# The clock that places pairs of scores among an FFN's passes: two constants for an exponential instead of one

## The chip, the cores and the metric

The kernel runs on one core of one Trainium2 chip. The metric is the device time of one execution in microseconds (us). Five engines take part: TensorE (PE in the profile; PEld is its loading of weights, which overlaps matmuls), VectorE (DVE), ScalarE (ACT), GpSimd (POOL) and SyncE (SP, which issues most DMAs). Each engine takes its own instructions in order, and waits on the others by semaphores.

## What is computed

One transformer layer on 2048 tokens of width 576: normalisation and attention with 32 query heads that share one key and value head of 18 columns, then a second normalisation and a bilinear FFN with 4608 hidden columns, both with a residual.

```
q = (x @ wq).reshape(B, S, H, Dh).transpose(0, 2, 1, 3)
k, v = x @ wk, x @ wv
scores = einsum("bhqd,bkd->bhqk", q, k) * (Dh ** -0.5)
p = softmax(scores, axis=-1)
o = einsum("bhqk,bkd->bhqd", p, v)
h = A_x + o.transpose(0, 2, 1, 3).reshape(B, S, H * Dh) @ wo      # x above is layernorm(A_x)
g = einsum("bsd,df->bsf", layernorm(h), w_gate)
u = einsum("bsd,df->bsf", layernorm(h), w_up)
out = h + einsum("bsf,fd->bsd", g * u, w_down)
```

## The kernel before

The tokens are cut into four blocks of 512 queries. Attention of a block is 8 groups of 4 heads; a group takes 16 tiles of 128 keys, and a tile takes two **pairs** of scores. A pair (`pair`, `scores`, L628 and L629) is two matmuls of 56 rows that run side by side, into one of two PSUM tiles `s` (128 x 1024), and one exponential on ScalarE from there into a tile `P` in SBUF, of which there are seven. There are 1024 pairs. **Values** (`values`, L633) are eight matmuls that read the two P tiles of a key tile and add into `acc`; one such visit ends the use of both P tiles. `flush` issues the visits that are due; `pend` holds the key tiles whose pairs are issued and whose values are not, `half` an odd pair.

The FFN of a block (`ffn`) goes over 36 tiles of 128 hidden columns, here called steps. A step has 27 **passes** (L991): two matmuls side by side, for the gate (`pg`) and the up half (`pu`), from 64 rows each. Weights and activations are split in a high and a low part, hence three products for each of nine chunks. ScalarE then copies `pg` to `g` (L1008), VectorE multiplies with `pu` to `hf` (L1013), and the result is split in high and low parts by casts on ScalarE and subtractions on VectorE (`room`, L92 and L93). After every second step a down product (`down`, L936, 42 matmuls on `y`) with a scheme of seven products for a two by two split follows one step late.

TensorE has 282 pairs done before the FFN of block 0 begins; the other 742 are put among the passes of blocks 0 and 1, since TensorE would otherwise have to wait for ScalarE's exponentials. When the last pair is out, blocks 2 and 3 run their passes without any (there the two halves are named `gu`).

Where a pair goes is decided when the program is written, by a clock in microseconds that the code keeps. `t_pe` is TensorE's time: 0.23 for a pass and for a pair, 0.893 for a visit of values, and so on. `t_act` is ScalarE's. `ends[n]` is the time at which pair n's exponential is held to be done, and so its PSUM tile to be free. Ahead of every pass `pace` asks `room_for_pair`: a pair n goes in when pair n - 2 is done by `t_pe`, and when fewer than eight pairs wait for their values. `paced` moves the clock after a pair. An eighth pair has no P tile until the next visit of values; it is kept in `late`, and its exponential's time is set in `flush`. Values are due behind the thirteenth pass of a step and behind the last; behind the seventh too, where a group's last key tile is the first due. After each group of visits the next two pairs go in at once, as both PSUM tiles are free by then.

Three casts on ScalarE are issued at fixed passes of a step: that of the first hidden half behind the sixth pass of odd steps (`left_first`, 128 x 256), that of the sums behind the ninth pass of even steps (`left_sums`, 128 x 1024), and attention heads at times behind the fifteenth (`run_aux`). ScalarE takes them in the order in which the code issues them, between exponentials.

Of the kernel before, what the change touches and what calls it, by code (L numbers as in the profile page):

```python
# [57 lines left out]
class Block:  # L58
# [545 lines left out]

    def paced(self, n):

        self.t_pe += T_PAIR
        if len(self.pend) * 2 + len(self.half) > P_BUFS + (self.p2 is not None):
            self.late[n] = len(self.late)
        else:  # L610
            self.t_act = self.ends[n] = max(self.t_act, self.t_pe) + T_EXP

    def room_for_pair(self):

# [21 lines left out]
    def flush(self, n):  # L636

        if n:
            self.t_pe += T_SWITCH
        for b, g, t, Ps in self.pend[:n]:  # L640
            self.t_pe += T_VISIT
            for k in sorted(self.late)[:2]:
                del self.late[k]
                self.t_act = self.ends[k] = max(self.t_act, self.t_pe) + T_EXP
            if t == 0:
                self.acc = self.ps_acc(b, g)
            self.values(self.acc, Ps, t)
            if t == NT - 1:
                os_ = self.os[g] = self.op.tile([P, TB], F32, tag="os", bufs=1, name=f"os{b}_{g}")
                self.dve.transpose(os_, self.acc)  # L650
                self.aux.insert(0, (self.round + 1, lambda b=b, g=g, o=os_: self.normalise(b, g, o), None))
        del self.pend[:n]
# [577 lines left out]

RATE = 2.3

T_PASS, T_PAIR, T_VISIT, T_SWITCH, T_EXP, T_DOWN = 0.23, 0.23, 0.893, 0.2, 1.05, 5.85
P_BUFS = 6

P1, P2, P3, P4, P5, P6, P7 = (0, 0), (1, 1), (6, 2), (2, 6), (3, 3), (4, 4), (5, 5)
# [128 lines left out]
```

## Time and profile before

| | us |
|---|---|
| median of three runs | 2394.43 (2392.9 to 2395.39) |
| the profiled execution | 2392.47 |
| its span, from the first to the last instruction | 2390.7 |

The profile is of one execution. A row of a group reads: line, engine, operation, tiles out<-in, shapes, count | busy us, mean ns of one | idle time ahead of them and what ended it. The chain of waits is the work that ended last, followed back; each of its rows has a start, the time it holds on the chain, and the work. The end of a matmul is modelled: a matmul that starts to load weights late is drawn longer, so a busy TensorE need not run at its peak.

### The profile page before, as it was taken

To read this page: it belongs to the slowest core of one execution; us is meant where nothing else is said; L and a number is where in the kernel's file an instruction comes from. 1 tells how busy PE (TensorE), PEld (TensorE's weight loads), DVE (VectorE), ACT (ScalarE), POOL (GpSimd) and SP (SyncE) were. 2 spreads that over 40 slices of the span, in tenths; PEclk is the share of its full clock that TensorE was granted. 3 is DMA by queue.
4 is the path that set the end of the run, shared out by engine and by line. 5 is a ranking of instruction groups with operands and counts; after the bars stand their busy time and mean duration, and the time that the engine had idled before them with its cause. 6 is when DMAs were issued, how large, how long until landed. Compare 5 with 4: busy or idle time off the path is not lost.

```text
span 2390.7 us, 46004 instructions
## 1 busy us (share of the span) xinstructions
PE 2335.7 (98%) x18102; PEld 1563.2 (65%) x18102; DVE 1168.8 (49%) x2047; ACT 1405.7 (59%) x1868; POOL 647.4 (27%) x802
## 2 busy tenths in 40 slices
PE   7999999999999999999999999999799999999999
PEld 5333344666666666666666566667687888888888
DVE  7565543334343453344444433334566656566565
ACT  6888877766776677666676777775122323233232
POOL 5445301212212212212212122122232433334333
PEclk9999999999999999999999999999899999999999
DMA  5778733323323323353333233233544554655543
GB/s 175 259 255 290 259 131 106 115 84 109 121 85 115 105 93 118 100 163 117 99 103 115 76 111 121 83 103 123 175 144 142 191 186 169 204 177 190 181 164 125
DMA packets 158289, 345.41 MB, mean 144 GB/s; under 512 B 16845, under 2 KB 48461, under 8 KB 158069
## 3 DMA queue, kind: packets, MB, share of 16 engines
q1 hardware_dynamic: 155333, 331.16, 42.3%
q0 software_dynamic: 2736, 11.26, 1.5%
q8 instruction: 145, 2.38, 0.4%
q14 instruction: 75, 0.61, 0.1%
HBM read 272.45 MB, written 55.67 MB: 137 GB/s over the span
## 4 chain that ended last, share of the span: by engine, by line
PE 83%; DVE 2%; issue 1%; ACT 1%; DMA 0%; POOL 0%; DVEq 0%; SPq 0%; ACTq 0%; POOLq 0%
PE gu L991 19%; PE pg L991 17%; PE y L936 17%; PE acc L633 15%; PE s L628 11%; PE yo L774 3%; PE pu L991 1%; PE y L894 1%; ACT P L629 1%; DVE room L93 0%; PE ye L894 0%; DVE hf L1013 0%; ACT g L1008 0%; DMA q<-q_dram 0%; DVE ws L93 0%
## 5 line engine op out<-in xcount | busy, mean ns | idle before, releaser
L629 ACT ACTIVATE P<-s 128x1024 f32<-128x1024 f32 x1024 | 992.3, 1027 | 337.1 <-PE s L628 290.1
L944 POOL TENSOR_TENSOR h<-h,tmp 128x288 f32<-128x288 f32 x408 | 316.3, 808 | 924.7 <-ACT tmp L943 924.1
L991 PE MATMUL pu<-X,ws 64*128 64x512 f32 x1890 | 524.0, 390 | 0.0
L991 PE MATMUL pg<-X,ws 64*128 64x512 f32 x1890 | 523.9, 390 | 0.0
L633 PE MATMUL acc<-P,V 128*32 128x512 f32 x4096 | 500.4, 600 | 0.1
L991 PE MATMUL gu<-X,ws 64*128 64x512 f32 x3996 | 470.7, 391 | 3.3 <-DMA X<-X 2.3
L628 PE MATMUL s<-q,kT 56*128 56x512 f32 x2048 | 431.4, 441 | 8.7 <-ACT P L629 4.5
L991 PEld LDWEIGHTS gu<-X,ws 64*128 64x128 f32 x3996 | 382.7, 185 | 81.4 <-issue 8.4
L936 PE MATMUL y<-wdo,room 128*128 128x288 f32 x2856 | 409.1, 300 | 0.9 <-DVE h L939 0.9
L936 PEld LDWEIGHTS y<-wdo,room 128*128 128x128 f32 x2856 | 386.8, 188 | 31.8 <-issue 24.4
L628 PEld LDWEIGHTS s<-q,kT 56*128 56x128 f32 x2048 | 183.3, 184 | 328.0 <-ACT P L629 177.5
L991 PEld LDWEIGHTS pg<-X,ws 64*128 64x128 f32 x1890 | 350.0, 186 | 69.8 <-issue 2.0
L939 DVE TENSOR_TENSOR h<-h,y 128x288 f32<-128x288 f32 x544 | 235.8, 454 | 246.1 <-PE y L936 242.4
L991 PEld LDWEIGHTS pu<-X,ws 64*128 64x128 f32 x1890 | 350.0, 186 | 3.0 <-DVE hf L1013 0.2
L943 ACT COPY tmp<-y 128x288 f32<-128x288 f32 x408 | 162.9, 400 | 261.4 <-PE y L936 247.5
L92 POOL CAST ws<-wr 128x1152 fp32r<-128x1152 f32 x144 | 168.4, 1171 | 502.8 <-PE pu L991 352.5
L1013 DVE TENSOR_TENSOR hf<-pu,g 128x512 f32<-128x512 f32 x70 | 48.4, 692 | 434.0 <-ACT g L1008 434.0
L633 PEld LDWEIGHTS acc<-P,V 128*32 128x32 f32 x4096 | 105.8, 109 | 236.1 <-issue 213.0
L93 DVE TENSOR_TENSOR ws<-wr,ws 128x1152 fp32r<-128x1152 f32 x144 | 196.8, 1367 | 61.3 <-POOL ws L92 61.3
L1008 ACT COPY g<-gu 128x512 f32<-128x512 f32 x74 | 43.7, 590 | 197.8 <-PE gu L991 197.8
L92 ACT CAST room<-hf 128x256 fp32r<-128x256 f32 (+1 forms) x144 | 75.1, 521 | 95.7 <-DVE hf L1013 95.5
L93 DVE TENSOR_TENSOR room<-S,room 128x1024 fp32r<-128x1024 f32 x68 | 83.3, 1225 | 91.8 <-ACT room L92 91.7
(171 smaller groups left out, 1474.7 us busy)
## 6 DMA issues: line engine op xcount, KB each, us to landing
wdo<-wd_dram SPq DMA_DIRECT2D x492, 288.0 KB
wr<-in_wgu_dram SPq DMA_DIRECT2D x144, 576.0 KB
wd_dram<-wd_room SPq DMA_DIRECT2D x20, 1008.0 KB
q<-q_dram SPq DMA_DIRECT2D x64, 216.0 KB
q_dram<-qs SPq DMA_DIRECT2D x16, 504.0 KB
X<-X SPq DMA_DIRECT2D x28, 256.0 KB
wd_dram<-wd_hi SPq DMA_DIRECT2D x7, 1008.0 KB
wd_dram<-wd_src SPq DMA_DIRECT2D x7, 1008.0 KB
```

What stands on the lines that cost most here:

```text
L92: (copy or self.cast)(hi, src)
L93: self.dve.tensor_tensor(lo, src, f32(hi), ALU.subtract)
L628: self.pe.matmul(s_[:, i], self.kT[o:o + 56, t * P:(t + 1) * P], q[o:o + 56, pr], start=True, stop=True)
L629: self.act.activation(p_, s_, AF.Exp, scale=SCALE)
L633: self.pe.matmul(acc[32 * j:32 * j + 32, :], self.V[:, t, :], Ps[j // 2][:, j % 2, :], start=(t == 0), stop=(t == NT - 1), skip_group_chec ...
L774: pe.matmul(y[:, :HD], m, k, start=(i == 0), stop=(i == len(ms) - 1))
L936: pe.matmul(y[:, :HD], m[:, t * P:(t + 1) * P], k, start=(first and j == 0), stop=(j == 2), skip_group_check=True)
L939: dve.tensor_tensor(hs, hs, y[:, :HD], ALU.add)
L943: act.copy(z, y[:, :HD])
L944: pool.tensor_tensor(hs, hs, z, ALU.add)
L991: pe.matmul(ps, w[o:o + 64, wk, c], X[o:o + 64, xk, c], start=(j == 0), stop=(j == 26))
L1013: dve.tensor_tensor(hf, pu, g, ALU.mult)
```

## The change

`paced` and `flush` now share a method, and one constant for an exponential becomes three. Before, an exponential was held to start when its pair's own 0.23 us were over (or the one ahead of it was done), and both ScalarE and the PSUM tile were held to be free 1.05 later. Now it is held to start 0.6 after the pair's start (or when ScalarE can take it), ScalarE can take the next one 0.92 after that, and the PSUM tile is free 1.09 after that. For a pair with ScalarE idle the tile is thus held free 1.69 after the pair's start, where it was 1.28; for exponentials one behind another the distance is 0.92, where it was 1.05. Nothing is computed otherwise, and no instruction is added or taken out.

```diff
     def paced(self, n):
 
+        ready = self.t_pe + T_READY
         self.t_pe += T_PAIR
         if len(self.pend) * 2 + len(self.half) > P_BUFS + (self.p2 is not None):
-            self.late[n] = len(self.late)
+            self.late[n] = ready
         else:
-            self.t_act = self.ends[n] = max(self.t_act, self.t_pe) + T_EXP
+            self.exp_ends(n, ready)
+
+    def exp_ends(self, n, ready):
+
+        start = max(self.t_act, ready)
+        self.t_act, self.ends[n] = start + T_EXP, start + T_FREE
@@ flush
             for k in sorted(self.late)[:2]:
                 del self.late[k]
-                self.t_act = self.ends[k] = max(self.t_act, self.t_pe) + T_EXP
+                self.exp_ends(k, self.t_pe + T_READY)
@@
-T_PASS, T_PAIR, T_VISIT, T_SWITCH, T_EXP, T_DOWN = 0.23, 0.23, 0.893, 0.2, 1.05, 5.85
+T_PASS, T_PAIR, T_VISIT, T_SWITCH, T_READY, T_EXP, T_FREE, T_DOWN = 0.23, 0.23, 0.893, 0.2, 0.6, 0.92, 1.09, 5.85
```

All other functions are as before, and so is the order of instructions up to the FFN of block 0. In its steps, and in those of block 1, the pairs stand at other passes. TensorE's order in two steps of block 0 that follow each other, before and after (`.` a pass, `S` a pair, `V` a visit of values, `D` a down product):

```
even step, before  ....S....S...S..VVSS....S....S...S...VVVSSDSS
even step, after   ......S...S...S.VVVSS......S...S...S..VVSSDSS
odd step, before   ....S....S...S..VVVSS....S....S...S...VVVSS
odd step, after    ......S...S...S.VVVVSS......S...S...S..VVSS
a step with one visit in its first half, before  ....S....S...S..VS.S...S....S...S...VVVVSSDSS
the same step, after                             ......S...S...S.VSS......S...S...S..VVVVSSDSS
```

Both orders have 742 pairs and 372 visits in this stage; the visits stand in 143 groups before and 145 after.

## The prediction

> **What bounds the kernel now.** I read the head of the page first, then the busy time by stage, then the score rows of the stage that the change touches, and last the chain of waits and ScalarE's order in single passes.
>
> ```profile
> span 2390.7 us, 46004 instructions
> PE 2335.7 (98%) x18102; PEld 1563.2 (65%) x18102; DVE 1168.8 (49%) x2047; ACT 1405.7 (59%) x1868; POOL 647.4 (27%) x802
> L629 ACT ACTIVATE P<-s 128x1024 f32<-128x1024 f32 x1024 | 992.3, 1027 | 337.1 <-PE s L628 290.1
> ...
> 385.00:1643.00 1258.00, 1254.04 (x9850) 781.68 (x9848) 495.98 (x895) 885.11 (x1125) 244.80 (x286) 1.00 0.34 106
> 1643.00:2049.00 406.00, 383.94 (x3021) 330.76 (x3022) 247.55 (x440) 111.67 (x218) 135.72 (x162) 0.97 0.50 166
> ```
>
> The windows' columns are span, busy PE, PEld, DVE, ACT and POOL with their instructions, the granted clock, DMA share and GB/s. The first stretch is the FFN of blocks 0 and 1, where the clock places pairs: 1258 us of 2390.7. PE is busy for 1254.04 of them, ScalarE for 885.11 (70%). So TensorE sets the time there, and ScalarE matters only where a pair arrives too early for it. By the busy column nothing is left to win; but a matmul that waits for its weights' semaphore is drawn longer, not idle. That shows here:
>
> ```profile
> L991 PE MATMUL pu<-X,ws 64*128 64x512 f32 x1873 | 519.3, 390 | 0.0
> L628 PE MATMUL s<-q,kT 56*128 56x512 f32 x1474 | 303.0, 435 | 2.3 <-ACT P L629 0.7
> ...
> L628 PE MATMUL s<-q,kT x1474: 385/394/502, 384.8 to 1642.2; 56*128 56x512 f32 x185
>   ACT P L629: 68.0, 156
> ```
>
> A pass takes 390 ns; a score matmul of the same 512 columns 435 in the mean, with a median of 394 and a highest of 502. There are thus two kinds, some 390 and some 495 ns; the mean puts (435 - 390) / 105 = 43% in the long kind, 318 of the 742 pairs in the instruction order of this stage. 174 of them follow values, down products or an output projection and pay for that change of work anyway. The other 144 come right behind passes. The last row, from the score line's waits, gives the cause: 156 times the weight load waited for an exponential. The chain of waits shows one half of a step of passes (start, time on the chain):
>
> ```profile
> 693.81 0.66 PE s L628 x4
> 694.47 0.23 PE pg L991
> ...
> 695.17 0.22 PE pg L991
> 695.39 0.00 PE pu L991
> 695.39 0.46 PE s L628 x2
> ...
> 696.79 0.23 PE s L628 x2
> ...
> 697.72 0.23 PE s L628 x2
> ...
> 698.63 0.97 PE acc L633 x5
> ```
>
> Two pairs, four passes, a pair that costs 0.46, four passes, a pair at 0.23, three passes, a pair at 0.23, three passes, values. A pair needs the score buffer of the pair two before it, and ScalarE beside this stretch reads:
>
> ```profile
> 694.28 4.80 ACT L629 ACTIVATE P<-s 128x1024 f32<-128x1024 f32 x5 [2.32 <-PE s L628]
> ...
> 650.99 2.86 ACT L629 ACTIVATE P<-s 128x1024 f32<-128x1024 f32 x3 [0.79 <-PE s L628]
> 653.72 0.41 ACT L92 CAST room<-hf 128x256 fp32r<-128x256 f32 x1
> 654.01 1.96 ACT L629 ACTIVATE P<-s 128x1024 f32<-128x1024 f32 x2
> ```
>
> The first exponential starts 0.47 after its pair (694.28 - 693.81) and ends at 695.31 with the 1.027 of the page's row. The pair at 695.39 was placed for about 695.2: the old clock lets an exponential start when the pair's 0.23 are over, frees the buffer 1.28 after the pair's start, and four passes pass its test too early. Back to back, exponentials start (2.86 - 1.03) / 2 = 0.92 apart, where the clock has 1.05; that is why it leaves a needless fourth pass later.
>
> **The change, part by part.** It adds and removes no instruction: 742 pairs and 372 visits of values stand in both orders, and each step of 27 passes keeps its pairs to within two. What moves is the place. Before, 131 pairs stand four passes behind a pair; now none does. 129 stand six passes behind, and 255 three (141 before).
>
> *The early pair.* Two passes more are 0.46. The wait in the row is some 0.13 and the restart 0.10, so the pair now comes about 0.33 later than it could first run: nothing of 0.23 is left. The next pair stands six, and one three passes on, at the same distance from the values as before or one pass nearer. Price of the old stall: 0.46 - 0.23 = 0.23 in the row above; at other places more:
>
> ```profile
> 651.18 0.23 PE pg L991
> ...
> 652.09 0.55 PE s L628 x2
> ...
> 1437.13 0.50 PE s L628 x2
> ```
>
> That is 0.27 to 0.32. I take 0.25, nearer the plain form, for 131 + 7 pairs (seven more stand one pass behind a single pair, as at 1437.13): 34.5 us. Ends: 131 x 0.23 = 30 and 144 x 0.27 = 39.
>
> *Casts that now come ahead.* ScalarE's order moves with the pairs. In odd steps the cast of the hidden half, issued after the sixth pass, stood behind the third exponential (653.72 above); now it stands ahead of it. It takes 654.01 - 653.72 = 0.29 of ScalarE. By hand for this step: exponentials at 650.99 and 651.91, cast at 652.82, third exponential at 653.11 to 654.14. The new third pair behind passes stands 6 + 3 + 3 passes and two pairs after 651.18, at 651.18 + 12 x 0.228 + 0.46 = 654.38, 0.24 after that end; the stalled pair at 695.39 stood 0.08 after its own, the free one at 696.79 0.57. Between these I take 0.08 a place; 32 places, 2.6 us. Ends: 0, and 0.2 each or 6.4. The Trainium skill ("TensorE: Matmul & The Clock Gate", Terms at the head, engine queue depth) has ScalarE's queue as strict FIFO, which speaks against this edit: a cast moved ahead cannot be passed. Were ScalarE free to pass it, this term would be nothing; the order in the rows agrees with the rule.
>
> In even steps the cast of the sums moves ahead of the fourth exponential:
>
> ```profile
> 1431.29 3.94 ACT L629 ACTIVATE P<-s 128x1024 f32<-128x1024 f32 x4 [0.94 <-PE s L628]
> 1435.12 1.04 ACT L92 CAST room<-S 128x1024 fp32r<-128x1024 f32 x1
> 1436.05 4.82 ACT L629 ACTIVATE P<-s 128x1024 f32<-128x1024 f32 x5
> ```
>
> It takes 1436.05 - 1435.12 = 0.93. From the first of the two pairs as zero: exponentials at 0.47 and 1.39; the third, whose pair comes at 0.66 + 6 x 0.228 = 2.03, at about 2.37; cast 3.29; fourth 4.22; fifth 5.14 to 6.17. The values begin one pass behind the last pair, at 4.33. Where two visits follow (0.90 each), the second pair behind them starts at 6.56, free. Where one visit follows, it starts at 5.33 + 0.33 = 5.66 and waits until 6.2, with the restart 0.6. There are six such steps: 3.6 us. Ends 2.4 and 4.5 (0.4 to 0.75 each).
>
> *Small ones.* Values now start in 145 groups, not 143, each with a change of work on both sides of some 0.3: 0.6. At the nine casts of attention heads and behind the first pairs of a block of tokens I allow 1.5 (0 to 3).
>
> *Sum.* 34.5 - 2.6 - 3.6 - 0.6 - 1.5 = 26 us, of which nothing is hidden, since PE bounds the stage. Ends: 30 - 6.4 - 4.5 - 0.6 - 3 = 15.5, and 39 - 0 - 2.4 - 0.6 - 0 = 36. The span goes from 2390.7 to 2364.7. The profiled execution took 2392.47, 1.77 more than its span, and lies 1.96 under the median of 2394.43. On the median the sum gives 2368.
>
> What follows moves along: after block 1 the chain has a wait that starts from work of this block,
>
> ```profile
> 1675.20 16.93 issue
> ...
> 1692.14 0.67 POOL L92 CAST wos<-wor 128x576 fp32r<-128x576 f32 x1 [16.95 <-DMA wor<-in_wo_dram]
> ```
>
> for output weights that SyncE loads behind block 1's stores. It starts sooner by as much and lasts as long. In this stretch the granted clock is 0.97 (against 1.00 ahead of it), 0.03 x 406 = 12 us of clock not granted. The Trainium skill (the same page, Part 1, What's actually happening) has the gate's window free-running, so a shift of 26 us may move where it bites; by it the sum could be off by one window of 3.4 us at half rate, an estimate of 1.7 us either way. No row here shows which.
>
> **The rivals.**
> - *All of it is won.* The casts find slack, and the new third pairs aren't late. For it: the pair at 696.79 had 0.57 and ran free. Against: the 0.93 cast leaves the single-visit steps no slack. Time 2394.4 - 36 = 2358 to 2362.
> - *The stall only moves.* The weight load's restart, 0.10, is paid by the first pair behind a stretch of passes whether or not it waits, and the odd and even casts cost their high ends: 30 - 14 - 11 = 5. For it: the load has to wait for its semaphore ahead of the matmul. Against: 696.79 and 697.72 cost just 0.23. Time 2380 to 2390.
> - *Slower: values wait for the newest exponential.* In the first half of a step the last pair now stands one pass ahead of the values, not two. Its exponential ends 0.34 + 1.03 = 1.37 after the pair; the values start 0.23 + 0.23 = 0.46 after it. If a group's first visit read it, each of 70 steps would lose 0.91, 64 us, against 34.5 gained: 2424. It decides from 0.5 us a step. Against: visits take the oldest pairs, and only a group of three reads the newest, in the second half of its third visit, 0.46 + 2 x 0.90 + 0.45 = 2.71 after the pair; behind the sums' cast the exponential ends 6.17 - 3.87 = 2.30 after it. It holds by 0.4, and values are all that PE has queued there, so a loss would be whole.
> - *It does nothing measurable.* A pair's wait is taken over by the next wait on ScalarE. Against: ScalarE is idle for 30% of the stage. 2394.
>
> **How the numbers follow.** The sum has 0.70, everything won 0.12, the stall that moves 0.08, nothing 0.04, slower 0.06. The likeliest time is 2368, its own range 2358 to 2379 from the ends of the sum. The rival of the moved stall lies above, up to 2390, so the range reaches to 2383; below, everything won ends at 2358, and a microsecond for the spread of the runs shown (2392.9 to 2395.39) makes 2357. A difference under 0.2%, 4.8 us, can't be told from no change here. Faster by more: 0.70 + 0.12 + 0.08 = 0.90; within: 0.04; slower: 0.06.
>
> **What would show it.** Right: score matmuls near 400 ns in the mean, about 180 rather than 318 pairs of the long kind; waits of the score line's weight load for an exponential well under 156 times; on the chain, pairs six passes behind two others at 0.23; the stretch of blocks 0 and 1 shorter by some 26 us, the later ones as long as before. Casts shown right: in odd steps a third pair at some 0.3, in six even steps a second pair behind a single visit at 0.8 or more. Wrong: values that wait for an exponential, a stretch of blocks 0 and 1 as long as before, or third pairs at 0.4 throughout.

## The result and the profile after

| | before, us | after, us |
|---|---|---|
| median | 2394.64 (2392.9 to 2395.39, 4 runs) | 2373.6 (2371.25 to 2376.71, 4 runs) |
| the profiled execution | 2392.47 | 2374.37 |
| its span | 2390.7 | 2372.5 |

The ratio is 0.9914, with a 95% interval of 0.9897 to 0.9931: 21 us faster, 16 to 25. Forecast were 26 us and 2368, with a range of 2357 to 2383.

First, where the time went. The gate matmuls `pg` exist only in steps with pairs, so the first and the last of them bound the stage that the change touches (a tile's own rows: median, first and last start). Before:

```profile
L991 PE MATMUL pg<-X,ws x1890: 383/390/499, 377.2 to 1638.9; 64*128 64x512 f32 x189
```

After, with the head of its page and the score rows of the stage:

```profile
span 2372.5 us, 46002 instructions
PE 2316.5 (98%) x18102; PEld 1580.9 (67%) x18102; DVE 1164.5 (49%) x2047; ACT 1400.3 (59%) x1868; POOL 648.0 (27%) x802
...
L997 PE MATMUL pg<-X,ws x1890: 383/388/502, 379.9 to 1619.8; 64*128 64x512 f32 x189
...
L634 PE MATMUL s<-q,kT 56*128 56x512 f32 x1488 | 293.7, 420 | 2.9 <-ACT P L635 2.4
...
L634 PE MATMUL s<-q,kT x1488: 383/391/503, 379.3 to 1623.1; 56*128 56x512 f32 x186
  ACT P L635: 32.2, 68
```

The stage took 1261.7 and takes 1239.9: 21.8 us less. Ahead of it the profiled execution after is 2.7 longer (379.9 against 377.2, where nothing differs), behind it 0.9. That is the 18.2 by which the spans differ; the medians differ by somewhat more. TensorE's share of busy time is as before, 98%, and yet the span is 18 us shorter: busy time held the waits. The mean score matmul fell from 435 to 420 ns; by the same working as before, (420 - 390) / 105 = 29% are of the long kind, 212 pairs where there were 318. That falls short of the forecast of 400 ns and some 180 pairs. The weight loads of scores wait 68 times for an exponential, not 156 times.

An even step after the change, on the chain of waits (the passes between left out) and on ScalarE:

```profile
1051.32 0.66 PE s L634 x4
...
1053.36 0.23 PE s L634 x2
...
1054.28 0.23 PE s L634 x2
...
1055.20 0.23 PE s L634 x2
...
1055.66 2.02 PE acc L639 x16
1057.68 0.66 PE s L634 x4
```

```profile
1051.84 2.88 ACT L635 ACTIVATE P<-s 128x1024 f32<-128x1024 f32 x3
1054.62 1.04 ACT L92 CAST room<-S 128x1024 fp32r<-128x1024 f32 x1
1055.56 1.94 ACT L635 ACTIVATE P<-s 128x1024 f32<-128x1024 f32 x2
```

The pair six passes behind two others costs 0.23, as do the two after it. But the two visits of values behind them take 2.02. Before, two visits took 1.85:

```profile
403.90 1.85 PE acc L633 x16
```

The fourth exponential starts at 1055.56, behind the cast, and ends at 1056.58. The weight loads of the second visit show what that does:

```profile
1056.47 0.12 PEld L639 LDWEIGHTS acc<-P,V 128*32 128x32 f32 x2 [0.31 <-issue]
...
1056.63 0.14 PEld L639 LDWEIGHTS acc<-P,V 128*32 128x32 f32 x4
```

A visit has a load for each of its four heads; `values` gives the first two heads the first P tile and the others the second. In the visit ahead all four start within 0.03 of each other, at 1055.59. Here two start at 1056.47 and the others at 1056.63, 0.05 after the exponential's end: the second P tile came 0.16 late. An odd step shows the other cast ahead (chain, then ScalarE):

```profile
1039.76 0.23 PE s L634 x2
...
1040.67 0.23 PE s L634 x2
...
1041.59 0.36 PE s L634 x2
```

```profile
1038.23 1.94 ACT L635 ACTIVATE P<-s 128x1024 f32<-128x1024 f32 x2 [1.95 <-PE s L634]
1040.06 0.41 ACT L92 CAST room<-hf 128x256 fp32r<-128x256 f32 x1
1040.35 2.87 ACT L635 ACTIVATE P<-s 128x1024 f32<-128x1024 f32 x3
```

The third pair's buffer is free when the first of the three exponentials ends, at 1041.39; the pair's own weight load starts just behind that, at 1041.44 (a start on the chain is the end of the piece ahead), and the pair pays 0.36 - 0.23 = 0.13, the restart and a little wait.

### The profile page after: what moved, and what is told of

It is laid out like the page before. It is cut to its first block, busy times and chain, and to the rows that moved or that the text cites. A ratio compares the mean times of both kernels' runs of the same rounds, so it can differ in the third digit from the quotient of the medians.

```text
span 2372.5 us, 46002 instructions
## 1 busy us (share of the span) xinstructions
PE 2316.5 (98%) x18102; PEld 1580.9 (67%) x18102; DVE 1164.5 (49%) x2047; ACT 1400.3 (59%) x1868; POOL 648.0 (27%) x802
## 4 chain that ended last, share of the span: by engine, by line
PE 79%; ACT 3%; DVE 2%; issue 2%; DMA 0%; POOL 0%; SPq 0%; ACTq 0%; DVEq 0%; POOLq 0%
PE gu L997 19%; PE y L942 17%; PE acc L639 15%; PE pg L997 14%; PE s L634 9%; PE pu L997 3%; ACT P L635 3%; PE yo L780 2%; PE y L900 1%; ACT room L92 0%; DVE room L93 0%; DVE hf L1019 0%; DMA q<-m_dram 0%; DVE h L781 0%; PE ye L900 0%
## 5 line engine op out<-in xcount | busy, mean ns | idle before, releaser
L639 PE MATMUL acc<-P,V 128*32 128x512 f32 x4096 | 506.4, 601 | 0.1
L634 PE MATMUL s<-q,kT 56*128 56x512 f32 x2048 | 419.9, 431 | 10.0 <-ACT P L635 6.2
```

What stands on the lines that cost most here:

```text
L634: self.pe.matmul(s_[:, i], self.kT[o:o + 56, t * P:(t + 1) * P], q[o:o + 56, pr], start=True, stop=True)
L639: self.pe.matmul(acc[32 * j:32 * j + 32, :], self.V[:, t, :], Ps[j // 2][:, j % 2, :], start=(t == 0), stop=(t == NT - 1), skip_group_chec ...
```

## The experiments

My theory: TensorE bounds the stage; the change removes the wait of the pair that came four passes behind two others; part of it is given back where a cast, now ahead of an exponential, makes values or a later pair wait. Rivals: the gain comes from the closer spacing of the other pairs, or what was given back has nothing to do with the casts. The constants in the edits below are the three that the change has for an exponential (the title speaks of two): when it starts behind its pair, when the next can start, when the buffer is free. Times are medians of four runs; the kernel before, on the same chips, had 2394.7 (first four experiments), 2396.02 (fifth to eighth) and 2396.05 (ninth).

**First: both casts behind the last pair of the half.**

```diff
-                    if j == (8 if on else 2) and todo and not plain(n_ - 2):
+                    if j == (12 if on else 2) and todo and not plain(n_ - 2):
                         self.left_sums()
...
-                    if j == 5 and k:
+                    if j == (12 if on else 5) and k:
                         self.left_first(n_ - 1, hid[0])
```

Expected: 

> The changed kernel, with its two casts (first hidden half, sums) issued behind the last pair of a step's first half instead of behind the sixth and the ninth pass. My theory: the part of the gain that was given back comes from these casts standing ahead of exponentials. In even steps the second or third visit then waits for its exponential (25 groups of values, 4.3 us in the changed kernel's trace) and the second pair behind a single visit (6 steps, 0.6 each, 3.6 us); in odd steps the third pair restarts late (some 32 places at 0.10, 3.2 us). Expected: the stretch from the first to the last pass with pairs falls from 1240 to about 1230 us, the time from 2373.6 to 2362 to 2365. Rival (the waits come from ScalarE being full, whatever the order): stretch 1239 to 1241, time 2372 to 2375.

Measured: 2363.59, ratio to before 0.9875 (0.9859 to 0.9892). The stage, and an even step on ScalarE and on the chain:

```profile
L997 PE MATMUL pg<-X,ws x1890: 383/388/499, 376.2 to 1606.2; 64*128 64x512 f32 x189
```

```profile
1044.18 4.71 ACT L635 ACTIVATE P<-s 128x1024 f32<-128x1024 f32 x5
1048.79 1.04 ACT L92 CAST room<-S 128x1024 fp32r<-128x1024 f32 x1
```

```profile
1047.99 1.85 PE acc L639 x16
1049.85 0.66 PE s L634 x4
```

The five exponentials run without a break, the cast fills the time of the values, and two visits take 1.85 again. The stage is 1230.0 long, 9.9 less than with the change alone. So the casts gave back some 10 us, as 4.3 + 3.5 + 2.7 of the table below would have it; the rival, that ScalarE is full whatever the order, falls.

**Second: values of even steps one pass later.**

```diff
-                        if j == 13 or j == 7 and f and self.pend and self.pend[0][2] == 0:
+                        if j == 14 - k or j == 7 and f and self.pend and self.pend[0][2] == 0:
```

Expected: 

> The changed kernel, with the values of even steps due one pass later in the middle of the step (behind the fourteenth pass, not the thirteenth); casts where they are. My theory: a visit reads both of its P tiles at its start, and the sums' cast makes that exponential end 0.17 (two visits) to 0.24 (three) too late; one pass of 0.23 hides nearly all: 4 us less there, and the 0.6 of the second pair behind a single visit falls to 0.35 (1.5 us). Expected: stretch 1240 to about 1234, time 2367 to 2369; in even steps no group of values longer than 1.86 (two visits) or 2.72 (three). Rival (those groups are longer for another reason, such as weights of the values loaded late): groups as long as before, time 2372 to 2375.

Measured: 2368.43, ratio 0.9895 (0.9879 to 0.9912).

```profile
L997 PE MATMUL pg<-X,ws x1890: 383/388/500, 377.0 to 1611.1; 64*128 64x512 f32 x189
```

The stage is 1234.1, as worked out. Of the 27 groups of values that were too long (4.3 us together) two are left, with 0.24. The second pair behind a single visit waits 0.37 where it waited 0.58. So the longer groups were a wait for a late exponential, not something in the values themselves.

**Third: five passes.**

```diff
-... T_READY, T_EXP, T_FREE, T_DOWN = ... 0.6, 0.92, 1.09, 5.85
+... T_READY, T_EXP, T_FREE, T_DOWN = ... 0.4, 1.0, 1.05, 5.85
```

Expected: 

> The changed kernel's code with constants 0.4, 1.0 and 1.05 (ready, next, free): the first pair behind two others stands five passes behind them, not four (before) or six (after), the next ones three passes on, and the casts stand behind the same exponentials as before the change. My theory: a pair five passes on comes 0.10 to 0.17 after its buffer is free, so it pays 0 to 0.06 of the restart and no wait, and nothing is given back by casts or values: of the 35 us of stalls before, some 4 to 6 stay. Expected: stretch 1262 (before) to about 1231 us, time 2363 to 2367, faster than the change. Rival (the gain needs the six passes, because the restart of the weight load is paid whole as soon as the wait isn't long over): 138 restarts of 0.10 stay, 14 us, stretch 1246 to 1250, time 2378 to 2382.

Measured: 2375.32, ratio 0.9919 (0.9902 to 0.9935): no better than the change, and between what the two theories gave. **Ninth: the same with the casts of the first experiment**, to see what of it was the casts.

Expected: 

> Five passes (third experiment: 2375 us, where 2363 to 2367 was expected) with the casts behind the last pair of a half (first experiment). It tells what five passes still pay. If the casts: in the third experiment six second pairs behind single visits wait 0.43 each and some nine third pairs 0.4 (6 to 7 us), and these go: 2367 to 2370, which would leave restarts of 0.06 at 61 first pairs (4 us) and passes that are a few ns longer behind them (3 us) as the difference to the first experiment. If the restarts alone cost it: 2373 to 2377 as before.

Measured: 2371.94, ratio 0.9898 (0.9881 to 0.9914), between the two ranges given. The stage and the waits of the scores' weight loads, of the third and of the ninth, and the waits of the first experiment:

```profile
L997 PE MATMUL pg<-X,ws x1890: 383/392/500, 378.4 to 1619.8; 64*128 64x512 f32 x189
...
  ACT P L635: 59.3, 241
```

```profile
L997 PE MATMUL pg<-X,ws x1890: 383/391/498, 381.2 to 1619.0; 64*128 64x512 f32 x189
...
  ACT P L635: 60.7, 240
```

```profile
  ACT P L635: 18.8, 33
```

With the casts away the stage falls from 1241.4 to 1237.8, not to the 1230.0 of six passes. At five passes the weight load still waits for its exponential 240 times, where six passes and the same casts have 33. First pairs pay 0.05 to 0.09 of restart at some 60 places, and the passes are a little longer, a median of 391 to 392 ns against 388. Third pairs pay 0.46 to 0.50 at seven places in the third experiment and at eight in the ninth. I had expected these to go with the casts, but each of them stands behind the cast of an attention head, which the ninth leaves where it was; what did go are the second pairs behind single visits. My estimate for the third experiment missed by 10 us: I had counted the restart of first pairs alone, and neither the other pairs nor the passes behind. The rival's whole restart of 0.10 isn't there either.

**Fifth: three passes**, the wait made larger.

```diff
-... T_READY, T_EXP, T_FREE, T_DOWN = ... 0.6, 0.92, 1.09, 5.85
+... T_READY, T_EXP, T_FREE, T_DOWN = ... 0.1, 1.05, 1.05, 5.85
```

Expected: 

> The changed kernel's code with constants 0.1, 1.05 and 1.05: the first pair behind two others stands three passes behind them, one fewer than before the change; 742 pairs, values in 138 groups. My theory: that pair now waits one pass, 0.23, longer in each of about 138 places, and the passes behind it can't make that up: stretch from the first to the last pass 1262 (before) to about 1290 us, time 2418 to 2426, slower than before. Rival (what the pair waits is made up later, since ScalarE is idle for 30% of the stage): stretch 1258 to 1266, time 2391 to 2398.

Measured: 2416.06, ratio 1.0088 (1.0071 to 1.0104): 20 us slower than before, where 22 to 30 were expected. Its scores' loads wait longer and more often, 272 times where the kernel before has 156:

```profile
  ACT P L635: 114.6, 272
```

A pass earlier costs about a pass a place: by the single matmuls' starts, a median of 0.48 at the early pair where it was 0.26. The rival, that the wait is made up later, falls. Together with six passes this is the wait's size in steps: a first pair at three, four and six passes (casts aside) gives 2416, 2395 and 2364.

**Fourth: the latency alone.**

```diff
-... T_READY, T_EXP, T_FREE, T_DOWN = ... 0.6, 0.92, 1.09, 5.85
+... T_READY, T_EXP, T_FREE, T_DOWN = ... 0.6, 1.05, 1.05, 5.85
```

Expected: 

> The latency alone: constants 0.6, 1.05 and 1.05, so an exponential starts later by the clock but the next one is still 1.05 behind. Pairs stand six passes behind a group of two and then three or four; each step holds fewer, so that 38 of the 742 pairs go to block 2, and values come in 156 groups more than before by 13. My theory: the stalls behind two pairs go here as well (the first pair stands six passes on), which is worth what it is in the change, less 13 changes of work of 0.3 (4 us) and what pairs in block 2 cost in new places: time 2374 to 2382. Rival (the gain comes from the closer spacing, three passes instead of four, and not from the first pair): time as before, 2392 to 2400.

Measured: 2368.08, ratio 0.9887 (0.987 to 0.9903). Its scores' loads wait for an exponential

```profile
  ACT P L635: 13.3, 35
```

35 times, where the kernel before has 156. So the waits go without the closer spacing, and the rival that the spacing removes them falls. The time is another matter: it is 6 us below what I expected, and faster than the whole change. Its mean granted clock was 0.999 where the change had 0.994, which pointed at the 38 pairs that it leaves for block 2. **Sixth and seventh: 38 pairs held back**, in the kernel of the first experiment and in the kernel before the change.

```diff
-        return self.more(NB - 1) and (n - 2 in self.ends ...
+        return self.more(NB - 1) and (self.blk > 1 or n < 2 * NT * NG * NB - 38) and (n - 2 in self.ends ...
...
     def ffn(self, b):
-        X, hid, todo = self.X, [], None
+        X, hid, todo, self.blk = self.X, [], None, b
```

Expected, on top of the first experiment's casts: 

> The kernel with the casts behind the last pair of a half (first experiment), and the last 38 pairs held back until block 2's FFN, as the latency alone had left them (fourth experiment). My theory: they fill the wait at block 2's start, in which PE has nothing else (16.9 us in the kernel before): 38 pairs and 19 visits are 28 us of PE, of which block 2 grows by only 14. Expected: time 2363.6 less 14, 2347 to 2352, and granted clock 1.00 at block 2's start. Rival (the fourth experiment was fast for its wider spacing, not for its pairs in block 2): 2361 to 2366.

Expected, on the kernel before: 

> The kernel before the change, with the last 38 pairs held back until block 2's FFN; its clock is as it was. My theory: the wait at block 2's start is filled whatever the clock: 2394.7 less 14, 2378 to 2383. Rival (the gain of the fourth experiment belongs to its clock): 2392 to 2397.

Measured: 2351.71, ratio 0.9817 (0.98 to 0.9833), and 2381.62, ratio 0.9941 (0.9924 to 0.9957): 12 us less than the first experiment, 14 less than before. So of the 26.6 us of the fourth experiment some 14 belong to the 38 pairs, and the latency alone is worth some 12, less than the change with its 21. In its trace 23 groups of values last longer than others of their size, 9.7 us together, with a load in them that waits for an exponential; in the change's it is 4.3 us. What the closer spacing adds was not measured by itself. The same 16 us of block 2, 20 after its transposes, in the changed kernel and in the sixth experiment (span, busy PE, PEld, DVE, ACT, POOL, granted clock, DMA):

```profile
1664.00:1680.00 16.00, 9.62 (x66) 7.54 (x62) 7.36 (x10) 2.49 (x5) 3.38 (x3) 0.82 0.67 244
```

```profile
1627.00:1643.00 16.00, 15.84 (x130) 8.24 (x130) 6.05 (x9) 11.94 (x15) 2.89 (x3) 1.00 0.48 163
```

In the first, PE has 9.62 us of work while the output weights come, and the granted clock is 0.82; in the second, pairs and values fill the stretch, and the clock stays at 1.00. So it is in the sixth experiment in the 20 us ahead (PE 19.89) and the 40 behind (38.85), where the changed kernel's clock is 0.99 and 0.91. The wait for the output weights is shorter too, though not gone, here in the first and in the sixth experiment:

```profile
1659.44 0.67 POOL L92 CAST wos<-wor 128x576 fp32r<-128x576 f32 x1 [16.94 <-DMA wor<-in_wo_dram]
```

```profile
1631.68 0.67 POOL L92 CAST wos<-wor 128x576 fp32r<-128x576 f32 x1 [13.05 <-DMA wor<-in_wo_dram]
```

How the 12 us divide between the filling, the clock and these 3.9 was not tried. **Eighth: 60 pairs held back**, the same edit with 60.

Expected: 

> As the sixth, with 60 pairs held back. My theory: what can be won is the wait of 17 us and no more, and 38 pairs fill most of it; the further 22 pairs cost in block 2 what they save in block 1: 2345 to 2352, within 0.2% of the sixth. Rival (every pair moved to block 2 saves some 0.38 us, as the 38 did): 2363.6 less 23, 2338 to 2343.

Measured: 2350.58, ratio 0.981 (0.9794 to 0.9827), 1 us from the sixth and within the spread of either: 38 pairs fill what there is, and the rival of a gain by every pair (2338 to 2343) falls. The sixth and the eighth are the fastest kernels of this study, some 22 us below the change.

## Why the prediction was right, and where it was off

Adding up over all pairs behind passes, by the starts of single matmuls in the traces, what the gap ahead exceeds 0.23 by and what the gap behind does (places with more than 0.05), and the same way for the rest:

| step of the prediction | predicted, us | measured, us |
|---|---|---|
| the early pair, removed | 34.5 (138 places) | 34.4 (131 places) |
| odd steps, third pair behind the cast | 2.6 (32 x 0.08) | 2.7 (31 places) |
| single visits in even steps, second pair | 3.6 (6 x 0.6) | 3.5 (6 x 0.58) |
| casts of heads and others | 1.5 | 0.1 (2.4 before, 2.5 after) |
| two more groups of values | 0.6 | not measured alone |
| values that wait for an exponential | 0 | 4.3 (27 groups) |
| output projections that wait for VectorE | 0 | 2.0 |
| passes that stand closer, a gain | 0 | 2.9 |
| left over | | 2.3 |

*The early pair.* The mechanism and its size held: the wait did not show as idle time (passes start 0.23 apart and are drawn 0.39 long, and the late pair 0.10 longer still), two passes more took it away, and one pass fewer (fifth experiment) made it larger.

*The casts.* Both moves were foreseen with their places. For odd steps and single visits the price was right to a tenth of a us; the first experiment took it back by moving the casts. The casts of heads were priced as a new cost, and they are not: before the change eight third pairs wait behind one (0.27 each), after it seven (0.33 each).

*Values that wait.* This is the step that failed, and the sign came that the prediction had named for being wrong. The rival on values had the cause right, a newest exponential too late for a visit behind it, but I excluded it with a wrong reading of a visit: I took the second P tile to be read in the second half of its visit, which left 0.4 of slack. The weight loads above show the second visit of two stopped at its start, for the second tile. It read the fourth pair's exponential 0.45 earlier than I had it. Taken so, the sum's own numbers give the wait: the fourth exponential ends at 4.22 + 1.03 = 5.25, and the second visit starts at 4.33 + 0.90 = 5.23, so there was no slack. It was 0.17 at two visits and 0.24 at three, 4.3 us in all, and not the 64 us of the rival, since visits ahead of the last one had their tiles. With it the sum is 26 - 4.3 = 22, against 21.8 by the stage and 21 by the medians.

*What else the sum lacked.* That 22 and 21.8 agree so well is in part luck, since two more terms were missing and the heads' 1.5 was not there. Loads of output projections wait 5.2 us for VectorE's additions (seven times), where they waited 1.4 (four times); the projections of the stage last 2.0 longer together, in the first experiment as well. In the other direction, two passes one behind the other start 0.2280 apart in the mean, where it was 0.2301: some 2.9 us over the stage, which is gained together with the early pair's wait (see the last section). So 34.4 - 2.7 - 3.5 - 0.1 - 0.6 - 4.3 - 2.0 + 2.9 = 24.1, and the stage has 21.8. Of the other 2.3, 0.5 are a single visit that waits for an exponential after the change and not before, in the first experiment too; the rest was not followed.

*The other rivals.* That all of it is won gave 2358 to 2362; with the casts moved as well (first experiment) it is 2363.6, so it was the casts that stood between, but for 2 us. That the stall only moves, 2380 to 2390, is out: the plain pairs run at 0.23. What follows the stage moved along as said, 751.8 behind it before (2390.7 - 1638.9) and 752.7 after. The estimate of 1.7 us for the clock's window, drawn from the Trainium skill ("TensorE: Matmul & The Clock Gate", Part 1), allows for 0.9 but no run here shows that it was this.

## What to carry to other kernels

Where TensorE reads as 98% busy, compare mean and median of one form of matmul: here a mean above the median was a wait drawn as work, and its count was in the waits of the weight loads. When a change moves instructions on one engine, write down the new order on the engine that it feeds, with each cast or copy that it now passes; what stands ahead of an exponential delays all that reads it. And look for a stretch where the bounding engine waits for something fixed, before filling work more tightly elsewhere: 38 pairs moved there were worth 12 to 14 us, more than half of the change.

## What the runs showed of the hardware

A score matmul whose weight load had waited took some 495 ns, not 390: 0.10 more than the wait, at every such place. To escape that, the buffer has to be free some time ahead: with five passes, pairs came 0.10 to 0.17 after it by my working and at some 60 places still paid 0.05 to 0.09; with six and the casts away (first experiment) none of them pays more than 0.05.

I had not expected that the passes behind a late pair stand further apart too. In the kernel before, the first two distances behind a late pair are 0.235 and 0.232 in the mean, behind the other pairs 0.230 and 0.227; over the whole stage the mean distance is 0.2301 there, 0.2280 after the change and 0.231 in the two kernels with five passes. Their cause was not tried. And the granted clock fell to 0.82 in a stretch where TensorE had work for 60% of it, and stayed at 1.00 where pairs filled it.
